# Half-block products of a two-FFN kernel: another form of the seven products, and their x operands made on VectorE

## The chip, the cores and the metric

The kernel runs on one core of a Trainium2 chip (trn2). The metric is the device time of one execution in microseconds (us), the median of several runs. The kernel before the change took 1739.53 us (three runs, 1736.28 to 1740.06).

## The reference, cut to what matters

```python
x = attention(q, k, v)               # chunks of 64 tokens, brought to 4608 tokens x 512
h = x @ w_in                         # first FFN: 512 -> 2048
r = maximum(h, 0); x = (s * r * r + b) @ w_out
h = x @ w2_in                        # second FFN: 512 -> 2048
g = h * (1 / (1 + exp(-1.702 * h)))
return g @ w2_out                    # 2048 -> 512, fp32
```

All is fp32. The kernel gets fp32 accuracy from TensorE by splitting each operand into a high part (rounded to TensorE's fp32r format) and a low part (the rest). A product of two split operands then takes three matmuls: low by high, high by high, high by low.

## The kernel before, in words

**Stages.** The 4608 tokens are nine blocks of 512. Attention and the first FFN run first; the first FFN's results go to DRAM (`y_dram`). Of the second FFN, block 0 is done in the plain way, and blocks 1 to 8 are done as four pairs by the class `Halves`. The four pairs are the program's last part, and the change touches only them.

**One pair.** A pair of token blocks and the weights are cut into halves, so that a matrix product becomes a 2 by 2 by 2 product of halves. Instead of eight half products it is made of seven, M1 to M7, of sums of halves (a form of Strassen's method). The sums of weights are made beforehand and lie in DRAM (`wi_sums`, `wo_sums`). The pair has two such products: the *first product* (x by w2_in, then the gate) and the *second product* (g by w2_out). In each, every one of the seven products M is 8 slices (`i`) by 2 times 3 matmuls of 128x512, so a pair has 2 x 336 matmuls of that size, and the four pairs 2688.

**First product** (`first`, `keep`, `quarter`, `gate`). Per slice `i` the seven products are accumulated in PSUM banks. M6 and M7 go on in the bank in which M1 was, and M3 in M5's. Between two products of one bank, ScalarE copies the bank's interim sum to SBUF (`keep`, L549) so that VectorE can add it later. The four quarters of g, "11", "12", "22" and "21", are each made of an addition from a bank (L562, L564, L568, L566), a sigmoid on ScalarE (L553) and a multiplication on VectorE (L554).

**Second product** (`operand`, `second`, `keep_out`, `result`). For each M and each `i`, an operand is split: the high part on ScalarE (L616), the low part on VectorE (L617), the sum of g halves that a later M needs on VectorE (L621, L623, L625, L627). Then six matmuls follow (L647), three for each output half `z`. Results are added on VectorE (L662, L664, L668, L670), transposed (L673) and written by SyncE (L677).

**x operands** (`load_x`, `x_split`, `operands_x`). For each half `k`, four tiles `xr` of 256 KB are loaded (L477). ScalarE makes the high parts (L492), GpSimd the low parts (L493) and the sums of halves (L502, L505, L508, L511). This work for the next pair lies in the second product of this pair, 24 and 15 plan units ahead.

**What sets the order.** Every step is entered with `at(time, step)`, a planned time in units of one product of a slice, and the steps are emitted in the order of these times. Every engine then works through its own instructions in their order, and a tile scheduler places waits on semaphores between engines. SyncE (SP) issues all DMAs in one queue: weights for the first product (`load_wi`, L520), for the second (`load_wo`, L600), and x (L477). A load into a buffer waits in that queue until the buffer is free. Buffers are few: 12 weight buffers `wi`, 7 operand buffers (3 `gh`/`gl`, 4 `op`), 10 `tmp`, and 8 PSUM banks (two "h", two "at", four "acc").

Of the kernel before, what the change touches and what calls it, by code (L numbers as in the profile page):

```python
# [16 lines left out]
P = 128  # L17
# [41 lines left out]
def chunk_attention_two_ffn(ctx, tc, q, k, v, w1_in, w1_out, s, b, w2_in, w2_out, out):  # L59
# [404 lines left out]

    class Halves:
# [24 lines left out]
        def x_split(self, m, k, src):  # L490
            self.x[m, k] = hi, lo = self.x_place(len(self.x))
            nc.scalar.activation(out=hi, in_=src, func=AF.Copy)  # L492
            nc.gpsimd.tensor_tensor(out=lo, in0=src, in1=hi.bitcast(F32), op=ALU.subtract)  # L493

        def operands_x(self, k):

            b11, b12, b22, b21 = (self.raw[k, a, c] for (a, c) in ((0, 0), (0, 1), (1, 1), (1, 0)))
            self.x_split("M1", k, b11)
            self.x_split("M2", k, b21)
            self.x_split("M3", k, b22)  # L500
            yield
            nc.gpsimd.tensor_tensor(out=b11, in0=b12, in1=b11, op=ALU.subtract)  # L502
            self.x_split("M5", k, b11)
            yield
            nc.gpsimd.tensor_tensor(out=b12, in0=b22, in1=b12, op=ALU.subtract)  # L505
            self.x_split("M7", k, b12)
            yield
            nc.gpsimd.tensor_tensor(out=b22, in0=b22, in1=b11, op=ALU.subtract)  # L508
            self.x_split("M6", k, b22)
            yield  # L510
            nc.gpsimd.tensor_tensor(out=b21, in0=b22, in1=b21, op=ALU.subtract)  # L511
            self.x_split("M4", k, b21)
# [10 lines left out]

        def first(self, i, m):

            key = {"M6": "M1", "M7": "M1", "M3": "M5"}.get(m, m)
            start = key == m
            if start:
                u = 2 * (i % 2)
                self.ps[i, key] = {  # L530
                    "M1": lambda: h_ps.tile([P, NB_MAX], F32, tag="h", name="m1"),
                    "M5": lambda: at_ps.tile([P, NB_MAX], F32, tag="at", name="m5"),
                    "M2": lambda: acc_ps.tile([P, NB_MAX], F32, tag=f"acc{u}", name="m2"),
                    "M4": lambda: acc_ps.tile([P, NB_MAX], F32, tag=f"acc{u + 1}", name="m4"),
                }[key]()
            w = self.wi[i][PLACE[m]]
            for k in range(HK):
                xh, xl = self.x[m, k]
                hi, lo = w[:, k, 0, :], w[:, k, 1, :]
                for a, (l_, r_) in enumerate(((lo, xh), (hi, xh), (hi, xl))):  # L540
                    nc.tensor.matmul(  # L541
                        out=self.ps[i, key], lhsT=l_, rhs=r_,
                        start=start and k == 0 and a == 0, stop=k == HK - 1 and a == 2,
                        skip_group_check=not start,
                    )

        def keep(self, i, m, name):
            self.kept[i, name] = t = tmp("kept")
            nc.scalar.copy(out=t, in_=self.ps[i, m])  # L549

        def gate(self, h):
            r = tmp("r")
            nc.scalar.activation(out=r, in_=h, func=AF.Sigmoid, scale=1.702)  # L553
            nc.vector.tensor_tensor(out=h, in0=h, in1=r, op=ALU.mult)  # L554

        def quarter(self, i, name):
            one, two = self.g[i]
            g = {"11": one[:, 0, :], "12": one[:, 1, :], "22": two[:, 0, :], "21": two[:, 1, :]}[name]
            ps = {m: self.ps[i, m] for m in ("M1", "M2", "M4", "M5") if (i, m) in self.ps}
            kept = {n: self.kept[i, n] for n in ("M1", "M5", "M16", "M167") if (i, n) in self.kept}  # L560
            if name == "11":
                nc.vector.tensor_tensor(out=g, in0=ps["M2"], in1=kept["M1"], op=ALU.add)  # L562
            elif name == "12":
                nc.vector.tensor_tensor(out=g, in0=ps["M5"], in1=kept["M16"], op=ALU.add)  # L564
            elif name == "21":
                nc.vector.tensor_tensor(out=g, in0=kept["M167"], in1=ps["M4"], op=ALU.subtract)  # L566
            else:
                nc.vector.tensor_tensor(out=g, in0=ps["M1"], in1=kept["M5"], op=ALU.add)  # L568
            self.gate(g)
# [4 lines left out]
        def plan_first(self):  # L574
            self.wi = {}

            def load(i):
                self.w = {}
                self.load_wi(i)
                self.wi[i] = self.w  # L580
            for i in range(HF):
                t = self.base + 3.5 * i
                at(t - 9, load, i)
                at(t, self.rooms_g, i)
                for n, m in enumerate(IN_ORDER):
                    at(t + 0.5 * n, self.first, i, m)
                at(t + 0.6, self.keep, i, "M1", "M1")
                at(t + 1.1, self.keep, i, "M5", "M5")
                at(t + 1.6, self.quarter, i, "11")
                at(t + 2.1, self.keep, i, "M1", "M16")  # L590
                at(t + 2.6, self.quarter, i, "12")
                at(t + 3.6, self.quarter, i, "22")
                at(t + 3.55, self.keep, i, "M1", "M167")
                at(t + 3.65, self.quarter, i, "21")
# [10 lines left out]
        def operand(self, n, i):  # L605
            m = OUT_ORDER[n]
            one, two = self.g[i]
            b11, b12, b22, b21 = one[:, 0, :], one[:, 1, :], two[:, 0, :], two[:, 1, :]
            src = {"M1": b11, "M2": b21, "M3": b22, "M5": b11, "M6": b22, "M7": b12, "M4": b21}[m]
# [9 lines left out]

            if m == "M1":  # L620
                nc.vector.tensor_tensor(out=b11, in0=b12, in1=b11, op=ALU.subtract)  # L621
            elif m == "M2":
                nc.vector.tensor_tensor(out=b12, in0=b22, in1=b12, op=ALU.subtract)  # L623
            elif m == "M3":
                nc.vector.tensor_tensor(out=b22, in0=b22, in1=b11, op=ALU.subtract)  # L625
            elif m == "M6":
                nc.vector.tensor_tensor(out=b21, in0=b22, in1=b21, op=ALU.subtract)  # L627
# [3 lines left out]
        def second(self, n, i):  # L631
            m = OUT_ORDER[n]
            key = {"M6": "M1", "M7": "M1", "M3": "M5"}.get(m, m)
            start = key == m
            hi, lo = self.op.pop((n, i))
            w = self.wo[n, i // 2]
            for z in range(2):
                if start and i == 0:
                    self.ps[key, z] = {
                        "M1": lambda: acc_ps.tile([P, NB_MAX], F32, tag=f"acc{z}", name="m1"),  # L640
                        "M5": lambda: at_ps.tile([P, NB_MAX], F32, tag="at", name="m5"),
                        "M2": lambda: h_ps.tile([P, NB_MAX], F32, tag="h", name="m2"),
                        "M4": lambda: acc_ps.tile([P, NB_MAX], F32, tag=f"acc{2 + z}", name="m4"),
                    }[key]()
                wh, wl = (w[:, i % 2, z, part, :] for part in range(2))
                for a, (l_, r_) in enumerate(((wl, hi), (wh, hi), (wh, lo))):
                    nc.tensor.matmul(  # L647
                        out=self.ps[key, z], lhsT=l_, rhs=r_,
# [4 lines left out]
        def keep_out(self, z):  # L653
            self.kept[z] = t = tmp("kept")
            nc.scalar.copy(out=t, in_=self.ps["M5", z])

        def result(self, name, z):
            ps = self.ps
            c = tmp("c")
            if name == "11":  # L660
                nc.vector.tensor_copy(out=c, in_=ps["M1", z])
                nc.vector.tensor_tensor(out=c, in0=ps["M2", z], in1=c, op=ALU.add)  # L662
            elif name == "12":
                nc.scalar.copy(out=c, in_=ps["M1", z])  # L664
                nc.vector.tensor_tensor(out=c, in0=ps["M5", z], in1=c, op=ALU.add)
            elif name == "21":
                nc.scalar.copy(out=c, in_=ps["M1", z])
                nc.vector.tensor_tensor(out=c, in0=c, in1=ps["M4", z], op=ALU.subtract)  # L668
            else:
                nc.vector.tensor_tensor(out=c, in0=ps["M1", z], in1=self.kept[z], op=ALU.add)  # L670
# [11 lines left out]
        def plan_second(self):  # L682
            self.wo = {}
            base = self.base + 3.5 * HF
            for n, m in enumerate(OUT_ORDER):
                for r in range(HF // 2):
                    at(base + 4 * n + r - 9, self.load_wo, n, r)
                for i in range(HF):
                    t = base + 4 * n + 0.5 * i
                    at(t - 1.8, self.operand, n, i)  # L690
                    at(t, self.second, n, i)
                done = base + 4 * n + 4
                for z in range(2):
                    if m == "M5":
                        at(done + 0.1, self.keep_out, z)
                    if m == "M2":
                        at(done + 0.1, self.result, "11", z)
                    if m == "M6":
                        at(done + 0.1, self.result, "12", z)
                    if m == "M7":  # L700
                        at(done + 0.1, self.result, "21", z)
                        at(done + 0.2, self.result, "22", z)
# [81 lines left out]
```

## Time and profile before

| | |
|---|---|
| median of three runs | 1739.53 us |
| the profiled execution's own time | 1740.82 us |
| its span (first to last instruction) | 1739.0 us |
| mean granted TensorE clock | 0.967 of full speed |
| busy: TensorE matmuls (PE) | 1623.5 us, 93%, 8864 matmuls |
| busy: VectorE (DVE) | 1236.7 us, 71% |
| busy: ScalarE (ACT) | 738.5 us, 42% |
| busy: GpSimd (POOL) | 485.0 us, 28% |

The shares are means over all stages. The pairs take the stretch from 1051.7 us to the end of the span. In that stretch the busy shares differ between the first products and the second ones, so it is read piece by piece. Matmuls overlap in TensorE's pipeline, so their listed durations (0.39 us) are longer than the step from one to the next; the step is what counts. In the trace a start time is in us from the span's start.

### The profile page before, as it was taken

The numbers are of one execution on the slowest core, as the hardware profiler recorded it, in microseconds if no ns is written. First come the engines' busy times: TensorE is split into PE (matmuls) and PEld (weight loads), VectorE is DVE, ScalarE is ACT, GpSimd is POOL, SyncE is SP. The second block draws the span as 40 slices with busy tenths as digits, with TensorE's granted clock in tenths as the row PEclk, the third lists the DMA queues.
The fourth block names the chain that finished last, engine by engine and source line by source line (L and its number), as shares of the span: only waits on it lengthen the run. The fifth ranks groups of instructions, "written<-read, shape, count | busy, mean of one in ns | idle before, by whom it ended". The sixth has DMA issues, their size and how long they took to land.

```text
span 1739.0 us, 24721 instructions
## 1 busy us (share of the span) xinstructions
PE 1623.5 (93%) x8864; PEld 1317.1 (76%) x8864; DVE 1236.7 (71%) x1804; ACT 738.5 (42%) x1226; POOL 485.0 (28%) x398
## 2 busy tenths in 40 slices
PE   4767999999999999999999999988999899889997
PEld 3555788888878888888888888776877687768785
DVE  6999876868787776868633324779568956885684
ACT  3545533334333433333344424554346334633552
POOL 3677422223222223222234313034004400430000
PEclk7888999999999999999999999998999899999998
DMA  8723454655555556644243424674767576757662
GB/s 188 200 79 87 104 129 122 152 134 148 128 155 130 137 137 162 168 122 128 79 128 97 130 77 146 198 243 117 224 193 242 144 202 188 240 151 204 191 214 53
DMA packets 407130, 263.81 MB, mean 152 GB/s; under 512 B 264160, under 2 KB 354272, under 8 KB 407008
## 3 DMA queue, kind: packets, MB, share of 16 engines
q1 hardware_dynamic: 407008, 262.23, 54.4%
q8 instruction: 70, 1.15, 0.3%
q14 instruction: 52, 0.43, 0.1%
HBM read 205.52 MB, written 56.62 MB: 151 GB/s over the span
## 4 chain that ended last, share of the span: by engine, by line
PE 71%; DVE 18%; DMA 4%; ACT 2%; issue 2%; SPq 2%; POOL 1%; DVEq 0%; ACTq 0%; POOLq 0%
PE acc L445 19%; PE h L402 19%; PE m L541 16%; PE m L647 13%; DVE pt L299 2%; DVE wo L625 1%; DVE op L617 1%; PE xT L307 1%; PE sc L273 1%; DVE r L411 1%; DVE gl L617 1%; DVE wo L568 1%; DVE wo L627 1%; DMA xr<-y 1%; ACT kept L549 1%
## 5 line engine op out<-in xcount | busy, mean ns | idle before, releaser
L402 PE MATMUL h<-xh,wi 128*128 128x512 f32 x1280 | 401.8, 396 | 8.8 <-ACT r L410 6.1
L445 PE MATMUL acc<-gh,wo 128*128 128x512 f32 x1152 | 361.0, 397 | 21.4 <-ACT gh L415 13.0
L402 PEld LDWEIGHTS h<-xh,wi 128*128 128x128 f32 x1280 | 242.4, 191 | 61.2 <-issue 9.4
L445 PEld LDWEIGHTS acc<-gh,wo 128*128 128x128 f32 x1152 | 218.0, 191 | 68.3 <-issue 9.5
L402 PE MATMUL h<-xl,wi 128*128 128x512 f32 x640 | 251.5, 394 | 0.0
L445 PE MATMUL acc<-gl,wo 128*128 128x512 f32 x576 | 224.8, 393 | 2.4 <-POOL gl L416 2.4
L411 DVE SCALAR_TENSOR_TENSOR r<-r,sb 128x512 f32<-128x512 f32 x144 | 135.8, 943 | 106.0 <-ACT r L410 105.5
L647 PE MATMUL m<-op,wi 128*128 128x512 f32 x768 | 194.7, 403 | 14.6 <-DVE op L617 12.2
L647 PEld LDWEIGHTS m<-op,wi 128*128 128x128 f32 x768 | 147.1, 194 | 53.2 <-DVE op L617 19.8
L419 DVE SCALAR_TENSOR_TENSOR gl<-r,sb,gh 128x512 fp32r<-128x512 f32 x128 | 127.3, 995 | 69.7 <-ACT gh L418 69.5
L541 PE MATMUL m<-xh,wi 128*128 128x512 f32 x512 | 160.8, 395 | 2.6 <-DVE wo L568 0.8
L418 ACT ACTIVATE gh<-r,sb 128x512 fp32r<-128x512 f32 x128 | 92.6, 724 | 165.8 <-DVE r L411 165.2
L493 POOL TENSOR_TENSOR xl<-xr,xh 128x512 fp32r<-128x512 f32 x32 | 49.3, 1557 | 399.1 <-PE m L647 259.1
L410 ACT ACTIVATE r<-h 128x512 f32<-128x512 f32 x144 | 85.1, 591 | 153.3 <-PE h L402 147.1
L402 PEld LDWEIGHTS h<-xl,wi 128*128 128x128 f32 x640 | 122.1, 191 | 25.9
L140 POOL TENSOR_TENSOR wm<-wm,wc 128x512 int32<-128x512 int32 x42 | 61.8, 1470 | 264.4 <-DVE wm L136 103.6
L299 DVE STREAM_TRANSPOSE pt<-p 32x256 f32<-32x256 f32 x288 | 125.6, 436 | 4.8
L553 ACT ACTIVATE r<-wo 128x512 f32<-128x512 f32 x128 | 80.7, 631 | 112.6 <-DVE wo L562 51.0
L445 PEld LDWEIGHTS acc<-gl,wo 128*128 128x128 f32 x576 | 108.5, 189 | 26.2 <-POOL gl L416 3.2
L647 PE MATMUL m<-gh,wi 128*128 128x512 f32 x384 | 119.7, 404 | 3.7 <-DVE wo L566 3.7
L554 DVE TENSOR_TENSOR wo<-wo,r 128x512 f32<-128x512 f32 x128 | 87.3, 691 | 46.4 <-ACT r L553 43.5
L617 DVE TENSOR_TENSOR op<-wo,op 128x512 fp32r<-128x512 f32 x128 | 99.7, 793 | 28.1 <-ACT op L616 28.0
(113 smaller groups left out, 2597.9 us busy)
## 6 DMA issues: line engine op xcount, KB each, us to landing
wi<-wo_sums SPq DMA_DIRECT2D x112, 512.0 KB, 4.1
wi<-wi_sums SPq DMA_DIRECT2D x96, 512.0 KB, 3.7
wi_sums<-wst SPq DMA_DIRECT2D x32, 448.0 KB, 3.6
wo_sums<-wst SPq DMA_DIRECT2D x32, 448.0 KB, 3.5
wst<-in_moe_w_in SPq DMA_DIRECT2D x21, 512.0 KB, 4.6
wst<-in_moe_w_out SPq DMA_DIRECT2D x21, 512.0 KB, 4.1
y<-ost SPq DMA_DIRECT2D x36, 256.0 KB, 3.1
wi<-wi_sums SPq DMA_DIRECT2D x32, 256.0 KB, 3.6
```

The costliest lines, as they stand in the source:

```text
L299: nc.vector.transpose(out=pt[r.start + ek * BK:r.start + (ek + 1) * BK, :, eq * BK:(eq + 1) * BK], in_=p[r.start + eq * BK:r.start + (eq + ...
L402: nc.tensor.matmul(out=ps, lhsT=w_[:, kk, :], rhs=x_, start=kk == 0 and a == 0, stop=kk == KD - 1 and a == 2,)
L410: nc.scalar.activation(out=r, in_=ps, func=AF.Relu)
L411: nc.vector.scalar_tensor_tensor(out=r, in0=r, scalar=s_ap, in1=r, op0=ALU.mult, op1=ALU.mult)
L418: nc.scalar.activation(out=gh, in_=r, func=AF.Identity, bias=b_ap)
L419: nc.vector.scalar_tensor_tensor(out=gl, in0=r, scalar=b_ap, in1=gh.bitcast(F32), op0=ALU.add, op1=ALU.subtract)
L445: nc.tensor.matmul(out=acc[m], lhsT=l_, rhs=r_, start=i == 0 and a == 0, stop=i == KF - 1 and a == 2)
L541: nc.tensor.matmul(out=self.ps[i, key], lhsT=l_, rhs=r_, start=start and k == 0 and a == 0, stop=k == HK - 1 and a == 2, skip_group_check= ...
L553: nc.scalar.activation(out=r, in_=h, func=AF.Sigmoid, scale=1.702)
L554: nc.vector.tensor_tensor(out=h, in0=h, in1=r, op=ALU.mult)
L617: nc.vector.tensor_tensor(out=lo, in0=src, in1=hi.bitcast(F32), op=ALU.subtract)
L647: nc.tensor.matmul(out=self.ps[key, z], lhsT=l_, rhs=r_, start=start and i == 0 and a == 0, stop=i == HF - 1 and a == 2, skip_group_check= ...
```

## The change

It has three parts, all in the class `Halves`.

1. The 22 subtractions per pair that make x operands (14 low parts, 8 sums of halves) run on VectorE instead of GpSimd.
2. Another form of the seven products: M1, M6, M7 and M4 all accumulate in one bank ("x", one of the four "acc" banks, number `i % 4`), M5 and M3 in a bank "d", M2 in a bank "b". Per slice ScalarE keeps three interim sums instead of four. The quarter "21" is now the bank "x" itself: its sigmoid and its multiplication read PSUM, and no addition is needed. The quarter "12" gets a subtraction of "11" behind it, which takes the place of the eight subtractions that followed M1's operands; M7's operand is M1's quarter after M6's subtraction.
3. The order and the times: the second product runs M1, M5, M6, M2, M7, M3, M4, the first product by a table of times (M4 of a slice comes behind two products of the next); operands are planned 3 units ahead instead of 1.8; of the results, "11" comes after M2, "22" after M7, "12" after M3, and "21" after M4, transposed straight from PSUM. Six copies of interim sums go to ScalarE, and there are no copies on VectorE.

The core of the diff:

```diff
-IN_ORDER = ("M1", "M5", "M2", "M6", "M3", "M4", "M7")
-OUT_ORDER = ("M1", "M5", "M2", "M3", "M6", "M4", "M7")
+BANK = {"M1": "x", "M6": "x", "M7": "x", "M4": "x", "M5": "d", "M3": "d", "M2": "b"}
+OUT_ORDER = ("M1", "M5", "M6", "M2", "M7", "M3", "M4")
...
+    def minus(to, one, two):
+        nc.vector.tensor_tensor(out=to, in0=one, in1=two, op=ALU.subtract)
...
-            nc.gpsimd.tensor_tensor(out=lo, in0=src, in1=hi.bitcast(F32), op=ALU.subtract)
+            nc.vector.tensor_tensor(out=lo, in0=src, in1=hi.bitcast(F32), op=ALU.subtract)
...
             self.x_split("M1", k, b11)
+            minus(b12, b12, b11)
+            yield
+            self.x_split("M5", k, b12)
+            minus(b12, b22, b12)
...
+        def bank(self, key, bank, *tags):
+            pool, tag = {"x": (acc_ps, tags[0]), "d": (at_ps, "at"), "b": (h_ps, "h")}[bank]
+            self.ps[key] = pool.tile([P, NB_MAX], F32, tag=tag, name=bank)
...
         def first(self, i, m):
+            key = i, BANK[m]
+            start = key not in self.ps
             if start:
+                self.bank(key, BANK[m], f"acc{i % KD}")
...
+        def quarter(self, i, name):
+            if name == "21":
+                h = self.ps[i, "x"]
+            else:
+                ps, kept = {"11": ("b", "M1"), "12": ("d", "M16"), "22": ("x", "M5")}[name]
+                h = g
+                nc.vector.tensor_tensor(out=h, in0=self.ps[i, ps], in1=self.kept[i, kept], op=ALU.add)
             r = tmp("r")
             nc.scalar.activation(out=r, in_=h, func=AF.Sigmoid, scale=1.702)
-            nc.vector.tensor_tensor(out=h, in0=h, in1=r, op=ALU.mult)
+            nc.vector.tensor_tensor(out=g, in0=h, in1=r, op=ALU.mult)
+            if name == "12":
+                minus(g, g, one[:, 0, :])
...
+                for n, m in ((0, "M1"), (0.5, "M5"), (1.5, "M6"), (2, "M2"), (2.5, "M3"), (3, "M7"), (4.5, "M4")):
+                    at(t + n, self.first, i, m)
...
         def second(self, n, i):
+                start = m in ("M1", "M5", "M2")
                 if start and i == 0:
+                    self.bank(key, BANK[m], f"acc{HK + z}")
...
+            if name == "21":
+                c = self.ps["out", z, "x"]
...
-                    at(t - 1.8, self.operand, n, i)
+                    at(t - 3, self.operand, n, i)
                     at(t, self.second, n, i)
-                done = base + 4 * n + 4
+                done = base + 4 * n + 4.1
                 for z in range(2):
+                    if m in ("M1", "M5", "M6"):
+                        at(done, self.keep_out, z, BANK[m], {"M6": "M16"}.get(m, m))
+                    else:
+                        at(done, self.result, {"M2": "11", "M7": "22", "M3": "12", "M4": "21"}[m], z)
```

How the change moves instructions is seen in the order of an engine's instructions: line, operation, out<-in, shape, xcount for repeated ones, and the engines or DMA queues on whose semaphores it waits.

TensorE where the second product of the first pair starts, before. `m1_10530` is M1's bank for z = 0 and `m1_10534` that for z = 1; `m1_10355` is a bank of the first product.

```order
L647 MATMUL m1_10530<-gh_10484,wi_10320 128x512 [waits DMAHW6_49,DVE_49]
L647 MATMUL m1_10530<-op_10550,wi_10362 128x512 [waits DMAHW0_49]
L541 MATMUL m1_10355<-xh_9508,wi_10164 128x512 [waits Activation_49]
L647 MATMUL m1_10530<-op_10580,wi_10390 128x512 [waits DMAHW1_49,Activation_49]
L647 MATMUL m1_10530<-op_10580,wi_10390 128x512 [waits DVE_49]
L647 MATMUL m1_10534<-gh_10484,wi_10320 128x512 [waits DVE_49]
```

The same place after the change. `x_10411` is the bank of the last slice (i = 7), `x_10505` M1's bank for z = 0 and `x_10509` that for z = 1.

```order
L542 MATMUL x_10411<-xh_9554,wi_10222 128x512 [waits Activation_49]
L637 MATMUL x_10505<-gh_10429,wi_10295 128x512 [waits DMAHW6_49,DVE_49]
L637 MATMUL x_10505<-gh_10455,wi_10315 128x512 [waits DMAHW7_49]
L637 MATMUL x_10505<-op_10471,wi_10315 128x512 x3
L637 MATMUL x_10505<-op_10482,wi_10341 128x512 [waits DMAHW0_49]
L637 MATMUL x_10505<-op_10513,wi_10362 128x512 [waits DMAHW1_49]
L542 MATMUL x_10411<-xh_9562,wi_10220 128x512 [waits DVE_49]
L637 MATMUL x_10509<-gh_10429,wi_10295 128x512 [waits DVE_49]
```

After the change, M1 for z = 0 (21 matmuls there) is followed by the first product's last M4 and then by M1 for z = 1. The latter's bank is acc3, which is also the bank of slice 7 (7 % 4 = 3), so its first matmul waits for VectorE's last reading of `x_10411`.

VectorE at that place before: quarters of the last slice (`wo_10433`, `wo_10434`) and low parts of second-product operands.

```order
L568 TENSOR_TENSOR wo_10434<-m1_10435,kept_10470 128x512 [waits Activation_49]
L566 TENSOR_TENSOR wo_10434<-kept_10540,m4_10502 128x512
L617 TENSOR_TENSOR gl_10695<-wo_10433,gh_10694 128x512 [waits PE_49,Activation_49]
L617 TENSOR_TENSOR gl_10707<-wo_9888,gh_10706 128x512 [waits PE_49,Activation_49]
L554 TENSOR_TENSOR wo_10434<-wo_10434,r_10543 128x512 [waits Activation_49]
```

VectorE there after the change. `wo_10410<-x_10411,r_10570` is the multiplication of quarter "21" of slice 7, the last reading of that bank; the rows L497 and L467 with `xl` and `xr` are x operands of the next pair.

```order
L561 TENSOR_TENSOR wo_10410<-x_10411,kept_10447 128x512 [waits PE_49]
L564 TENSOR_TENSOR wo_10409<-wo_10409,r_10501 128x512 [waits Activation_49]
L467 TENSOR_TENSOR wo_10409<-wo_10409 128x512 [waits DVE_49]
L564 TENSOR_TENSOR wo_10410<-wo_10410,r_10519 128x512 [waits Activation_49]
L497 TENSOR_TENSOR xl_10633<-xr_10551,xh_10632 128x512 [waits DMAHW1_49,Activation_49]
L467 TENSOR_TENSOR xr_10553<-xr_10553,xr_10551 128x512 [waits DMAHW2_49]
L497 TENSOR_TENSOR xl_10676<-xr_10553,xh_10675 128x512 [waits Activation_49]
L564 TENSOR_TENSOR wo_10410<-x_10411,r_10570 128x512 [waits Activation_49]
L467 TENSOR_TENSOR xr_10553<-xr_10555,xr_10553 128x512 [waits DMAHW3_49,DVE_49]
```

After the change, three x instructions stand on VectorE ahead of that multiplication, the first of which waits for a load of x. These x instructions were GpSimd's before.

SyncE's queue around the loads of x for the second pair, before and then after.

```order
L600 DMA wi_10727<-wo_sums_138 128x1024 [waits DMAHW6_49,PE_49]
L477 DMA xr_10572<-y3_142 128x512 [waits DMAHW7_49,DVE_49,Pool_49]
L477 DMA xr_10574<-y4_143 128x512 [waits DMAHW0_49,DVE_49]
L477 DMA xr_10576<-y4_143 128x512 [waits DMAHW1_49,DVE_49]
L477 DMA xr_10578<-y3_142 128x512 [waits DMAHW2_49,DVE_49]
L600 DMA wi_10756<-wo_sums_138 128x1024 [waits DMAHW3_49,PE_49]
```

```order
L597 DMA wi_10549<-wo_sums_138 128x1024 [waits DMAHW0_49,PE_49]
L481 DMA xr_10551<-y3_142 128x512 [waits DMAHW1_49,DVE_49,Activation_49]
L481 DMA xr_10553<-y4_143 128x512 [waits DMAHW2_49,DVE_49]
L481 DMA xr_10555<-y4_143 128x512 [waits DMAHW3_49,DVE_49]
L481 DMA xr_10557<-y3_142 128x512 [waits DMAHW4_49,DVE_49]
L597 DMA wi_10583<-wo_sums_138 128x1024 [waits DMAHW5_49,PE_49]
```

The loads of x stand six weight loads earlier in the queue than before, right behind the load of `wi_10549`, which waits on TensorE for a buffer that the first product's last M7 reads.

## Rows read from the trace of the kernel before

**Rows 1.** The page's part 4: the chain that ended last, by line.

```profile
PE acc L445 19%; PE h L402 19%; PE m L541 16%; PE m L647 13%; DVE pt L299 2%; DVE wo L625 1%; DVE op L617 1%; PE xT L307 1%; PE sc L273 1%; DVE r L411 1%; DVE gl L617 1%; DVE wo L568 1%; DVE wo L627 1%; DMA xr<-y 1%; ACT kept L549 1%
```

**Rows 2.** Instructions of two matmul lines: duration ns, then first and last start.

```profile
L541 PE MATMUL m<-xh,wi x512: 386/390/505, 1051.7 to 1663.1; 128*128 128x512 f32 x171
...
L647 PE MATMUL m<-op,wi x768: 387/390/797, 1129.5 to 1726.1; 128*128 128x512 f32 x192
```

**Rows 3.** The chain of waits: start us, us, what; three runs of matmuls.

```profile
1056.85 23.59 PE m L541 x104
...
1081.88 8.48 PE m L541 x36
...
1091.80 8.51 PE m L541 x36
```

**Rows 4.** Windows: stretch, length, busy us (x instructions) by engine, PEclk, DMA share, GB/s.

```profile
1160.00:1193.00 33.00, 24.31 (x82) 17.27 (x81) 31.45 (x25) 15.18 (x28) 29.72 (x18) 0.84 0.45 146
...
1226.00:1300.00 74.00, 73.47 (x318) 58.90 (x317) 50.69 (x78) 34.79 (x61) 0.00 (x0) 1.00 0.69 201
...
1335.00:1365.00 30.00, 22.42 (x69) 15.67 (x67) 29.96 (x24) 11.27 (x20) 27.24 (x17) 0.77 0.39 121
...
1508.00:1538.00 30.00, 20.14 (x68) 13.57 (x67) 29.96 (x25) 11.29 (x20) 26.43 (x16) 0.89 0.38 116
```

**Rows 5.** Timeline of DVE, then of POOL, in the first of these stretches.

```profile
1167.23 1.77 DVE L617 TENSOR_TENSOR op<-wo,op 128x512 fp32r<-128x512 f32 x1
1168.93 1.77 DVE L627 TENSOR_TENSOR wo<-wo 128x512 f32<-128x512 f32 x1
...
1168.41 1.74 POOL L493 TENSOR_TENSOR xl<-xr,xh 128x512 fp32r<-128x512 f32 x1
```

**Rows 6.** Timeline of DVE in the second pair's first product, where POOL rests.

```profile
1265.63 0.68 DVE L623 TENSOR_TENSOR wo<-wo 128x512 f32<-128x512 f32 x1
1266.23 0.68 DVE L562 TENSOR_TENSOR wo<-m,kept 128x512 f32<-128x512 f32 x1
```

**Rows 7.** Instructions of two DVE lines: duration ns min/median/max, first and last start.

```profile
L625 DVE TENSOR_TENSOR wo<-wo x32: 676/1168/1775, 1165.6 to 1691.3; 128x512 f32<-128x512 f32 x32
...
L662 DVE TENSOR_TENSOR c<-m,c x8: 677/678/683, 1182.4 to 1692.5; 128x512 f32<-128x512 f32 x8
```

**Rows 8.** The chain of waits at the start of the first pair's second product.

```profile
1132.72 0.60 ACT kept L549
...
1133.34 0.69 DVE wo L568
1134.03 0.60 DVE wo L566
```

**Rows 9.** Loads of x: landing of all; of two bursts, with the median.

```profile
DMA to landing us min/median/max: 4.6/6.7/8.1
...
xr<-y SPq DMA_DIRECT2D x4, 256.0 KB, 7.2
...
xr<-y SPq DMA_DIRECT2D x4, 256.0 KB, 5.0
```

**Rows 10.** Instructions of two ACT lines, the high part of x and the sigmoid.

```profile
L492 ACT ACTIVATE xh<-xr x32: 613/631/636, 991.7 to 1516.8; 128x512 fp32r<-128x512 f32 x32
...
L553 ACT ACTIVATE r<-wo x128: 615/632/637, 1062.0 to 1667.2; 128x512 f32<-128x512 f32 x128
```

**Rows 11.** Windows inside the first stretch of rows 4.

```profile
1170.50:1174.10 3.60, 0.22 (x1) 0.00 (x0) 3.60 (x4) 2.24 (x5) 3.60 (x3) 0.87 0.47 148
1174.10:1180.00 5.90, 5.46 (x12) 3.68 (x12) 5.90 (x5) 1.46 (x3) 5.90 (x4) 0.50 0.00 1
...
1183.40:1186.80 3.40, 3.40 (x10) 2.59 (x9) 3.40 (x4) 1.16 (x2) 2.26 (x3) 0.50 0.00 0
```

**Rows 12.** Timeline of the end of the program.

```profile
1727.93 8.67 SPq L677 DMA_DIRECT2D out<-ost  x16
...
1731.15 0.71 DVE L673 STREAM_TRANSPOSE ost<-c 128x512 f32<-128x512 f32 x1
```

More of the change, by code (lines that the diff above doesn't have):

```diff
@@ L498, in operands_x @@
             self.x_split("M1", k, b11)
+            minus(b12, b12, b11)
+            yield
+            self.x_split("M5", k, b12)
+            minus(b12, b22, b12)
+            yield
+            self.x_split("M6", k, b12)
+            minus(b11, b12, b11)
+            yield
             self.x_split("M2", k, b21)
+            minus(b21, b21, b12)
+            yield
+            self.x_split("M7", k, b11)
             self.x_split("M3", k, b22)
[L501 to L511, printed above, removed]
             self.x_split("M4", k, b21)
@@ L545, in first, with keep @@
                     )
[L547 to L553, printed above, removed]
-            nc.vector.tensor_tensor(out=h, in0=h, in1=r, op=ALU.mult)
+        def keep(self, key, name):
+            self.kept[key[0], name] = t = tmp("kept")
+            nc.scalar.copy(out=t, in_=self.ps[key])
         def quarter(self, i, name):
@@ L584, in plan_first @@
                 at(t, self.rooms_g, i)
[L585 to L591, printed above, removed]
+                for n, m in ((0, "M1"), (0.5, "M5"), (1.5, "M6"), (2, "M2"), (2.5, "M3"), (3, "M7"), (4.5, "M4")):
+                    at(t + n, self.first, i, m)
+                at(t + 0.6, self.keep, (i, "x"), "M1")
+                at(t + 1.1, self.keep, (i, "d"), "M5")
+                at(t + 2.1, self.keep, (i, "x"), "M16")
+                at(t + 2.6, self.quarter, i, "11")
+                at(t + 3.1, self.quarter, i, "12")
                 at(t + 3.6, self.quarter, i, "22")
-                at(t + 3.55, self.keep, i, "M1", "M167")
-                at(t + 3.65, self.quarter, i, "21")
+                at(t + 5.1, self.quarter, i, "21")
         def load_wo(self, n, r):
@@ L607, in operand @@
             one, two = self.g[i]
-            b11, b12, b22, b21 = one[:, 0, :], one[:, 1, :], two[:, 0, :], two[:, 1, :]
-            src = {"M1": b11, "M2": b21, "M3": b22, "M5": b11, "M6": b22, "M7": b12, "M4": b21}[m]
+            b11, t1, b22, b21 = one[:, 0, :], one[:, 1, :], two[:, 0, :], two[:, 1, :]
+            src = {"M1": b11, "M2": b21, "M3": b22, "M5": t1, "M6": t1, "M7": b11, "M4": b21}[m]
             if self.n_ops % 7 < 3:
@@ L618, in operand @@
             self.op[n, i] = hi, lo
[L620 to L621 removed]
+            if m == "M5":
+                minus(t1, b22, t1)
+            elif m == "M6":
+                minus(b11, t1, b11)
             elif m == "M2":
[L623 to L627, printed above, removed]
+                minus(b21, b21, t1)
         n_ops = 0
@@ L651, in second, with keep_out @@
                     )
-        def keep_out(self, z):
-            self.kept[z] = t = tmp("kept")
-            nc.scalar.copy(out=t, in_=self.ps["M5", z])
+        def keep_out(self, z, bank, name):
+            self.kept[z, name] = t = tmp("kept")
+            nc.scalar.copy(out=t, in_=self.ps["out", z, bank])
         def result(self, name, z):
[L658 to L668, printed above, removed]
-            else:
-                nc.vector.tensor_tensor(out=c, in0=ps["M1", z], in1=self.kept[z], op=ALU.add)
+            if name == "21":
+                c = self.ps["out", z, "x"]
+            else:
+                ps, kept = {"11": ("b", "M1"), "12": ("d", "M16"), "22": ("x", "M5")}[name]
+                c = self.kept[z, kept]
+                nc.vector.tensor_tensor(out=c, in0=self.ps["out", z, ps], in1=c, op=ALU.add)
             o = tmp("ost").rearrange("p (u l) -> p u l", l=BK)
```

43 lines of the change are left out of this document (5 added, 38 removed).

## The prediction

> **What bounds the kernel now.** I read the chain that ended last first, by line [rows 1]. The reader is to see that the pairs' part of it is TensorE's (L541 16%, L647 13%) with pieces of VectorE (L625, L617, L627) in between. Next I asked how long the pairs' matmuls must take. They run from 1051.7 to 1726.1 [rows 2], 674.4 us. In an unbroken run 104 of them take 23.59 us, 0.2268 each [rows 3]. There are 2688, and 12 of an earlier stage lie among them: 2700 x 0.2268 = 612.3 us. So **62.1 us of that stretch are lost**, and 12.9 more lie between the last matmul and the end of the span (1739.0).
>
> Where they go is read from the windows by stage [rows 4]. In three stretches, one in the second product of each of the first three pairs, TensorE does 82, 69 and 68 matmuls in 33, 30 and 30 us: 14.4 + 14.3 + 14.6 = 43.3 us lost. VectorE is busy there for 31.4, 30.0 and 30.0 us, thus nearly always, and GpSimd for about 27 to 30. In a stretch without GpSimd (1226 to 1300) VectorE is busy for 50.69 of 74 us and TensorE for 73.47.
>
> The timeline shows why [rows 5]: while GpSimd makes x operands, each subtraction of two SBUF tiles takes 1.77 us on VectorE and 1.74 on GpSimd, and VectorE starts one each 1.70 us (1167.23 to 1168.93). Without GpSimd it takes 0.68, and the next starts 0.60 later [rows 6]. L625 shows both ends, 0.68 to 1.78 us [rows 7], while L662, one of whose inputs is in PSUM, stays at 0.68 throughout. So in these stretches VectorE is the bound, and what slows it is GpSimd beside it.
>
> **The change part by part.**
>
> *x operands to VectorE.* Removed: 22 GpSimd subtractions per pair, 66 in the three pairs that have this work in a second product (the first pair's lie earlier, in a stretch where I cost the move at nothing, since TensorE has other blocks' matmuls ready). A VectorE and a GpSimd operation together took 1.70 us; two on VectorE take 2 x 0.60 = 1.20. A second product then has on VectorE 56 low parts, 24 sums of g, 22 x operations, 6 additions and 8 transposes: 116 x 0.60 = 69.6 us, against 336 x 0.2268 = 76.2 us on TensorE. TensorE is the longer one, so the three stretches' 43.3 us go. At 0.69 an operation, the longest that rows show for one without GpSimd, VectorE would need 80 us and lose 3.8 per pair. No row shows an x operation on VectorE; nearest are the equal SBUF subtractions at 0.60, so I take that, with 0.69 as the other end.
>
> *Four products in one bank.* Before, TensorE loses at slice hand-overs: from 1081.88 to 1091.80 it has 42 matmuls, 9.53 us, and needs 9.92, so 0.39 a slice [rows 3], about 2.4 in a first product. After, by the order, three products of other banks lie between M1 and M6 and between M6 and M7 (4.1 us), and one between M7 and M4 (6 x 0.2268 = 1.36 us). The addition that must read the bank in between takes 0.69 [rows 8], with the matmul's tail (0.39 less 0.23) and two issues about 0.95: covered. At one place per pair (slice 6) M7 and M4 stand back to back: 0.95 lost. I leave in one of the old hand-overs, 0.4. The two steps give 1.35 per pair. An edit with one answer goes with it: a copy fewer on ScalarE per slice and an addition exchanged for a subtraction on VectorE, off the path, since neither engine fills the first product.
>
> Here a rule speaks against the change. The trace shows a price of a hand-over only where ScalarE's copy (0.60) and VectorE's addition (0.69) follow each other [rows 8]. The Trainium skill, PSUM — Partial Sum Buffer, "PSUM bank collisions raise a hardware error", says that two engines on one bank must be held apart by semaphores since the hardware doesn't arbitrate; so each product in the shared bank waits for its reader. By that rule the fourth product adds eight waits per pair; were none covered, 32 x 0.95 = 30 us would be lost. By the order it is covered, and the sum goes by that.
>
> *The start of the second product.* This is a **new wait**. Let P be the end of the last M7. By the order, TensorE then has 21 matmuls of M1 (z = 0) and 6 of M4: 27 x 0.2268 = 6.1 us. M1 for z = 1 waits for VectorE's multiplication of quarter 21, slice 7, because both use acc3. That multiplication stands on VectorE behind three x operations, and these wait for a load of x. That load stands in SP's queue behind a weight load that waits for P, so it is issued at about P + 0.6. Loads of x land 4.6 to 8.1 us after issue, median 6.7, bursts 5.0 and 7.2 [rows 9]; I take 6.2, nearer the quieter burst, as fewer weight loads are in flight there. Then come: high part 0.63, low part and sum 2 x 0.60, second high part 0.63, sigmoid 0.63 [rows 10], multiplication 0.69, with hand-overs 4.1. TensorE goes on at P + 0.6 + 6.2 + 4.1 = P + 10.9, thus **4.8 us late** (3.2 with a landing of 4.6, 6.7 with 8.1). Queued behind the waiting low part are the next low parts of g, but those have M1 z = 1's matmuls ahead of them.
>
> After a hold the clock may fall: behind 3.6 us in which one matmul ran, the granted clock was 0.50, the lower of the two levels (1.2 of 2.4 GHz); 12 matmuls took 5.9 us, 3.2 too long; another such piece did 10 in 3.4, 1.1 too long [rows 11]. I take 2.0 per hold. So 6.8 per pair in the first three pairs. The fourth has no next pair: its multiplication needs only sigmoid, multiplication and issues behind M4, 1.6.
>
> *The end.* Four results become two, and these are transposed straight from PSUM. Now 16 DMA issues take 8.67 us, 0.54 each, and the span ends 2.4 after them [rows 12]. After, the last matmul starts at E; z = 0's transposes start before it, so the 8 issues start at about E + 0.5, end at E + 4.8, and the span at E + 7.2 instead of E + 12.9: **5.7 less**. A transpose from PSUM is not in the trace; I take the 0.71 of one from SBUF [rows 12]. An addition that reads PSUM costs 0.68 like one that doesn't [rows 6, 7], so I see no end that moves the sum by more than 0.1.
>
> **Sum.** Loss in the pairs after: 3 x (1.35 + 6.8) + 1.35 + 1.6 = 27.4 instead of 62.1, thus 34.7 less; with the end 40.4 less. The profiled execution took 1740.8 (span 1739.0 and 1.8 around it): 1700.4. It lies 1.3 above the median of the runs, so I predict **1699 us**. The forecast's own range, from a landing of 8.1 (+5.7) and some operations at 0.65 to short holds, is 1692 to 1709.
>
> **Rivals.**
>
> *A. The new wait is short and the clock stays up.* With the landing of 4.6 the hold is 3.2, and without the clock's 2.0 each pair saves 3.6 more: 1699 - 3 x 3.6 = **1688**. For it: one load burst landed in 5.0. Against: the loads run beside 512 KB weight loads, and the hold is then hardly shorter than the one behind which the clock fell [rows 11]. The Trainium skill, DMA: Bandwidth & Descriptors, "Anatomy of one DMA — SWDGE (gpsimd) path", gives a fixed part of about 2.0 us plus the bytes at 436 GB/s, which for 256 KB is an estimate of 2.6 us; no load of x here landed so early. Were the hold only the fourth pair's 1.6 with no clock lost: 1699 - 3 x 5.2 = 1683.
>
> *B. VectorE becomes the bound of the second product.* The x work is a chain in turn on ScalarE and VectorE. If VectorE stands for each of 8 high parts and their hand-overs (0.7 each, 5.6 us per pair) and an operation costs 0.65: 116 x 0.65 + 5.6 = 81.0 against 76.2, 4.8 lost per pair, 1699 + 14.4 = **1713**; at 0.69 even 1727. For it: VectorE has only 9% to spare over the whole product and the x work lies in one half of it. Against: the operands are planned earlier (3 units), and in a stretch without GpSimd it kept TensorE at 99% [rows 4].
>
> *C. The shared bank decides: slower.* If at each M7 to M4 the reader is late (behind other VectorE work in its queue), TensorE stands there 28 times. The place is the addition of quarter 22. It decides from 1.45 us per hand-over on, where 28 x 1.45 = 40.6 eats all of the gain; at 1.8 it gives 28 x 1.8 = 50, **1749**. It needs the addition to end 3.2 us after M7. For it: every x bank waits twice for VectorE. Against: VectorE was busy for only 69% of a first product [rows 4].
>
> *D. The change doesn't do what it says*: VectorE's slow subtractions had another cause than GpSimd, for instance DMA traffic, so 1.70 stays, and now 22 more come. It would come out near **1740**. Against: L625's shortest and longest differ by exactly GpSimd's presence [rows 6, 7].
>
> **How the numbers follow.** Forecast 0.62, A 0.14, B 0.18, C 0.04, D 0.02. The range of 8 in 10 takes in the forecast, most of A and the nearer half of B: 1683 to 1717. Two runs of this kernel can be told apart from about 0.2% on, 3.5 us. Faster by more than that: forecast, A and B, 0.94; within: D, 0.02; slower: C, 0.04.
>
> **What would show it.** In the profile after: no GpSimd work beyond about 1050 us; VectorE's subtractions at 0.68 throughout; windows in the middle of a second product with TensorE at 99%; a hold of 3 to 7 us about 6 us into each of the first three second products, released by the multiplication of L564, with a granted clock of 0.5 behind it; the first products within 1.5 us of 76.2; and 7 us between last matmul and end. The forecast is wrong if VectorE is busy through a second product with TensorE waiting for low parts of g (L615 in the changed kernel, B), or if TensorE's holds in first products are released again and again by the additions of quarters (L561 there, C).

## The result, and the profile after

The changed kernel took **1697.38 us** (median of four runs, 1696.16 to 1698.30) against 1739.41 before: a ratio of 0.9761, 95% interval 0.9745 to 0.9778. The forecast was 1699, its own range 1692 to 1709.

The profiled execution (1696.5 us of span, 1739.0 before) is best read in three pieces, by the start times of matmuls:

| piece | before | after | difference | forecast |
|---|---|---|---|---|
| up to the pairs' first matmul | 1051.7 | 1049.9 | -1.8 | 0 |
| first to last matmul of the pairs | 674.4 | 639.5 | -34.9 | -34.7 |
| last matmul's start to the end | 12.9 | 7.1 | -5.8 | -5.7 |

The first line is no effect of the change that I can name: in eight more kernels, alike up to the pairs but for the first pair's x work, the pairs began between 1048.4 and 1051.9. The other two are 40.7 us against a forecast of 40.4.

The page of the changed kernel, engines and chain by line. GpSimd is 139 us lighter (485.0 before), and the VectorE lines L617, L625 and L627 of [rows 1] have no successors among the lines of the chain that the page lists:

```profile
PE 1603.6 (95%) x8864; PEld 1317.1 (78%) x8864; DVE 1198.1 (71%) x1844; ACT 722.8 (43%) x1194; POOL 345.6 (20%) x310
...
PE acc L446 21%; PE h L403 21%; PE x L637 10%; PE x L542 10%; PE d L637 5%; PE d L542 5%; PE b L637 3%; PE b L542 2%; DVE pt L300 2%; PE xT L308 2%; PE sc L274 1%; DVE r L412 1%; DMA xr<-y 1%; DMA wst<-in_moe_w_in 1%; SPq L246 1%
```

Windows of the changed kernel (columns as in [rows 4]): the middle of the first and the second pair's second product, and between them a first product. These answer to [rows 4]:

```profile
1145.00:1191.00 46.00, 46.00 (x205) 38.06 (x204) 44.78 (x75) 28.08 (x49) 0.00 (x0) 1.00 0.72 221
1211.00:1289.00 78.00, 77.22 (x341) 63.61 (x340) 44.88 (x68) 33.70 (x59) 0.00 (x0) 1.00 0.73 218
1304.00:1351.00 47.00, 47.00 (x208) 38.86 (x207) 45.88 (x77) 29.48 (x52) 0.00 (x0) 1.00 0.73 224
```

In the middle pieces TensorE now never rests, where before it did 82 matmuls in 33 us. VectorE is just as full as before (44.78 of 46, 45.88 of 47), but it does 75 instructions there where it did 25 in 33 us. The sums of halves in the changed kernel, by instruction, answer to L625 in [rows 7]:

```profile
L467 DVE TENSOR_TENSOR wo<-wo x128: 676/682/693, 1067.6 to 1650.3; 128x512 f32<-128x512 f32 x128
```

None of 128 takes over 0.69 us. Next, the new wait: the chain of waits of the changed kernel at the start of the first pair's second product (start us, us, what):

```profile
1129.13 6.32 DMA xr<-y
...
1135.48 0.64 ACT xh L496
...
1136.14 0.69 DVE xl L497
1136.83 0.61 DVE xr L467
...
1137.47 0.64 ACT xh L496
...
1138.13 0.52 DVE xl L497
...
1138.74 0.69 DVE wo L564
...
1139.47 8.11 PE x L637 x25
```

The load lands 6.32 us after its issue (6.2 was taken), then come high part (L496), low part (L497), sum (L467), high part, low part and the multiplication of L564, 4.0 us where the forecast had 4.1. The forecast counted the sigmoid where the chain names the second low part; it ran beside that on ScalarE:

```profile
1138.00 0.58 ACT L563 ACTIVATE r<-x 128x512 f32<-128x512 f32 x1
```

Then TensorE goes on with M1 for z = 1. From the start times of the matmuls, this hold is 4.83 us, in the second and third pair 5.15 and 5.04, in the fourth 1.57 (forecast 4.8 and 1.6). Windows around it, the same columns:

```profile
1134.40:1139.40 5.00, 0.40 (x2) 0.00 (x0) 2.56 (x5) 1.75 (x3) 0.00 (x0) 0.78 0.56 188
1139.40:1144.04 4.64, 4.57 (x11) 3.60 (x12) 4.61 (x9) 3.70 (x7) 0.00 (x0) 0.50 0.13 24
```

Behind the hold the granted clock is 0.50, that is 1.2 of 2.4 GHz, and 11 matmuls take 4.64 us where 20 fit.

The end of the program after the change, DVE and SP (answering to [rows 12]):

```profile
1689.13 1.40 DVE L656 STREAM_TRANSPOSE ost<-x 128x512 f32<-128x512 f32 x2 [6.60 <-PE x L637]
1689.88 4.14 SPq L660 DMA_DIRECT2D out<-ost  x8
```

Two transposes straight from the bank and 8 DMA issues, 7.1 us from the last matmul's start (1689.4) to the end (1696.5).

### The profile page after: what moved, and what is told of

The parts are those of the page before. It is cut to its first block, busy times and chain, and to the rows that moved or that the text cites. A ratio compares the mean times of both kernels' runs of the same rounds, so it can differ in the third digit from the quotient of the medians.

```text
span 1696.5 us, 24510 instructions
## 1 busy us (share of the span) xinstructions
PE 1603.6 (95%) x8864; PEld 1317.1 (78%) x8864; DVE 1198.1 (71%) x1844; ACT 722.8 (43%) x1194; POOL 345.6 (20%) x310
## 4 chain that ended last, share of the span: by engine, by line
PE 79%; DVE 12%; DMA 3%; SPq 2%; ACT 1%; issue 1%; POOL 0%; DVEq 0%; ACTq 0%; POOLq 0%
PE acc L446 21%; PE h L403 21%; PE x L637 10%; PE x L542 10%; PE d L637 5%; PE d L542 5%; PE b L637 3%; PE b L542 2%; DVE pt L300 2%; PE xT L308 2%; PE sc L274 1%; DVE r L412 1%; DMA xr<-y 1%; DMA wst<-in_moe_w_in 1%; SPq L246 1%
## 5 line engine op out<-in xcount | busy, mean ns | idle before, releaser
L614 ACT ACTIVATE op<-wo 128x512 fp32r<-128x512 f32 x128 | 79.9, 631 | 80.9 <-PE x L637 27.8
L564 DVE TENSOR_TENSOR wo<-wo,r 128x512 f32<-128x512 f32 x96 | 66.0, 691 | 63.4 <-ACT r L563 62.9
L637 PE MATMUL x<-op,wi 128*128 128x512 f32 x432 | 104.9, 390 | 0.0
L542 PE MATMUL x<-xh,wi 128*128 128x512 f32 x320 | 99.6, 391 | 3.3 <-DVE wo L561 3.1
L637 PEld LDWEIGHTS x<-op,wi 128*128 128x128 f32 x432 | 81.7, 189 | 17.3
L563 ACT ACTIVATE r<-wo 128x512 f32<-128x512 f32 x96 | 60.7, 633 | 76.5 <-DVE wo L561 75.8
L615 DVE TENSOR_TENSOR op<-wo,op 128x512 fp32r<-128x512 f32 x128 | 85.3, 680 | 7.4 <-ACT op L614 6.0
L467 DVE TENSOR_TENSOR wo<-wo 128x512 f32<-128x512 f32 x128 | 85.7, 684 | 0.8
```

The lines of the kernel that those rows point to most:

```text
L467: nc.vector.tensor_tensor(out=to, in0=one, in1=two, op=ALU.subtract)
L542: nc.tensor.matmul(out=self.ps[key], lhsT=l_, rhs=r_, start=start and k == 0 and a == 0, stop=k == HK - 1 and a == 2, skip_group_check=not ...
L615: nc.vector.tensor_tensor(out=lo, in0=src, in1=hi.bitcast(F32), op=ALU.subtract)
L637: nc.tensor.matmul(out=self.ps[key], lhsT=l_, rhs=r_, start=start and i == 0 and a == 0, stop=i == HF - 1 and a == 2, skip_group_check=not ...
```

## The experiments

Eight kernels were run. "Loss" below is the time of a stretch less 0.2268 us per matmul in it, from start times.

| kernel | median us | ratio to before, 95% interval |
|---|---|---|
| x subtractions on VectorE, else as before | 1704.04 | 0.9805 (0.9788 to 0.9822) |
| changed kernel, x subtractions on GpSimd | 1736.08 | 0.9988 (0.9978 to 0.9997) |
| changed kernel, other bank for M1 | 1679.79 | 0.9669 (0.9651 to 0.9687) |
| changed kernel, x loaded earlier | 1689.53 | 0.9718 (0.9699 to 0.9736) |
| changed kernel, lead 1.8 | 1697.81 | 0.9773 (0.9758 to 0.9787) |
| changed kernel, low parts of x twice | 1705.69 | 0.9808 (0.9793 to 0.9822) |
| other bank, x 2 units earlier | 1677.70 | 0.9648 (0.9632 to 0.9664) |
| other bank, x 4 units earlier | 1680.36 | 0.9665 (0.9650 to 0.9679) |

**One: only the engine of the x work.** The kernel before, with

```diff
-            nc.gpsimd.tensor_tensor(out=lo, in0=src, in1=hi.bitcast(F32), op=ALU.subtract)
+            nc.vector.tensor_tensor(out=lo, in0=src, in1=hi.bitcast(F32), op=ALU.subtract)
```

and the same in the four sums of `operands_x`.

> The kernel before with one thing changed: the 22 x subtractions per pair run on VectorE instead of GpSimd; form, banks and order stay. Theory (GpSimd's operations beside VectorE's are what stretched these to 1.70 us): no VectorE subtraction of the pairs over 0.75 us, and most of the 43 us of the three middle stretches go. This form needs 128 VectorE operations in a second product, 128 x 0.60 = 76.8 us against TensorE's 76.2, so some 10 to 15 us stay: 1705 to 1716. Rival (the new form and order freed the stretches, or the stretch has another cause than GpSimd): 1730 or more, with L617 and L625 still at 1.7 us.

Measured: 1704.04, a little under the range given. Windows of this kernel in the first pair's second product, and L625 there:

```profile
1150.00:1172.00 22.00, 22.00 (x99) 18.13 (x98) 19.53 (x34) 14.65 (x27) 0.00 (x0) 1.00 0.92 315
1172.00:1186.00 14.00, 10.82 (x43) 7.38 (x42) 14.00 (x24) 5.73 (x10) 0.00 (x0) 1.00 0.61 155
```

```profile
L625 DVE TENSOR_TENSOR wo<-wo x32: 674/682/692, 1163.4 to 1652.2; 128x512 f32<-128x512 f32 x32
```

L625, 1.78 us at its longest before, is 0.69 at its longest, with the line, its operands and the form of the seven products untouched: GpSimd beside it was the cause. The DMA share beside it is even higher (0.92) than in the slow stretches of [rows 4]. What stays is a piece of 14 us in which VectorE is busy throughout and TensorE does 43 matmuls: 128 operations are one more than TensorE's 76.2 us hold at 0.60 (127). The Trainium skill, SBUF — State Buffer, "Who interferes with whom", states that a VectorE instruction with two SBUF inputs contends with a GpSimd one that reads SBUF, and one with at most one SBUF input, outside the 2-port modes, does not. The trace agrees: 1.70 against 0.60 a step, while L662, with one input in PSUM, stayed at 0.68 [rows 5 to 7], also where a GpSimd subtraction ran beside it (kernel before):

```profile
1182.37 0.68 DVE L662 TENSOR_TENSOR c<-m,c 128x512 f32<-128x512 f32 x1
...
1181.98 1.62 POOL L505 TENSOR_TENSOR xr<-xr 128x512 f32<-128x512 f32 x1
```

**Two: only the form.** The changed kernel with the 22 subtractions back on GpSimd (`nc.gpsimd` in `x_split` and for the four sums in `operands_x`).

> The changed kernel with the x subtractions back on GpSimd; form, banks, order and lead stay. Theory: the 1.70 us operations come back in the second products of the first three pairs, some 11 to 14 us lost in each, less 2 to 4 for the wait at the start of the second product, since VectorE no longer stands behind a load of x there: 1715 to 1730. Rival (the form and the longer lead carry the gain): within 5 us of 1697.

Measured: 1736.08, outside the range: the theory's direction, but more came back than expected. The loss in the second products is 20.6, 20.4 and 18.6 us, the wait at their start included. Timeline of this kernel, DVE then POOL, and its chain of waits:

```profile
1150.12 1.75 DVE L618 TENSOR_TENSOR op<-wo,op 128x512 fp32r<-128x512 f32 x1
...
1149.62 1.71 POOL L470 TENSOR_TENSOR xr<-xr 128x512 f32<-128x512 f32 x1
```

```profile
1141.63 3.48 DVE gl L618 x2
...
1145.11 5.09 DVE wo L467 x3
1150.20 1.67 DVE op L618
...
1155.30 2.85 PE d L640 x8
...
1183.73 1.55 issue
1185.29 1.74 DVE wo L467
1187.03 1.68 DVE gl L618
```

VectorE steps at 1.70 us again, and this time in two bursts per pair, as the loads of the two halves come apart; in the first two pairs the granted clock fell to 0.50 once in each burst. The range took 11 to 14 us per pair for this, but these rows show VectorE on the path from 1141.6 on, with nothing to cover it. The wait at the start shrank to 3.3, 3.0 and 2.5 us only, since the sigmoid on ScalarE still stood behind a high part of x that waits for the load.

The first two kernels and the two given ones make a square: with x on GpSimd the new form brings 2.6 us (1738.69 to 1736.08), with x on VectorE 6.7 (1704.04 to 1697.38); the move to VectorE brings 34.7 with the old form and 38.7 with the new. (1738.69 is the kernel before in these experiments' session; it was 1739.41 in the changed kernel's, and by the intervals each of these differences is known to some 3 to 4 us.) The end of the program alone gives 5.9 of the form's share (12.97 us in experiment one, 7.09 after the change). So **in the pairs themselves the new form gained nothing**: the loss there is 26.2 us in experiment one's profiled execution and 27.1 after the change. It saved 1.3 us in each first product (losses 2.3 to 2.6 against 1.1 to 1.5) and what VectorE lacked in the second, and gave it back in the wait for the bank. Without that wait the same form does bring something: experiment three, below, is 24.3 us faster than experiment one.

**Three: another bank.** The changed kernel with M1 for z = 0, 1 in the second product in acc1 and acc2:

```diff
-                    self.bank(key, BANK[m], f"acc{HK + z}")
+                    self.bank(key, BANK[m], f"acc{1 + z}")
```

> The changed kernel with M1's banks in the second product moved from acc2 and acc3 to acc1 and acc2, so that M1 for z = 1 no longer shares a bank with slice 7 of the first product. The planner then also orders the instructions there anew (x operands later on VectorE). Theory (the 5 us wait of each second product is one for that bank): the waits and the half clock behind them go, some 7 us in each of three pairs and 1.6 in the fourth: 1672 to 1680. Rival (TensorE needs VectorE's work there in any case, and the wait comes back at the next low part): 1688 to 1700.

Measured: 1679.79, at the upper end of the theory's range. Neither hold nor half clock is left at the starts of the second products, and the 0.95 of the back-to-back M7 and M4 is gone too: the planner now puts M1 of the second product between them, and a first product loses nothing that the start times show. The planner's new order is not what frees TensorE: the multiplication of quarter 21, slice 7, comes later than before, 1151.44 where it was 1138.74, and no matmul waits for it:

```profile
1151.44 0.67 DVE L564 TENSOR_TENSOR wo<-x,r 128x512 f32<-128x512 f32 x1
```

Windows of the first pair's second product:

```profile
1120.00:1135.00 15.00, 15.00 (x68) 12.41 (x67) 9.54 (x15) 8.26 (x16) 0.00 (x0) 1.00 0.62 180
1135.00:1174.00 39.00, 37.63 (x167) 30.82 (x165) 39.00 (x66) 24.23 (x43) 0.00 (x0) 1.00 0.84 274
1174.00:1187.00 13.00, 11.75 (x50) 9.42 (x51) 12.96 (x22) 7.80 (x15) 0.00 (x0) 1.00 0.44 134
```

Part of the rival came true: VectorE is busy without a pause from 1135 on, and late in the product TensorE waits for it, 3 us a pair, by way of copies of interim sums on ScalarE (L645) that stand behind high parts of x. With the hold gone the x work in turn on ScalarE and VectorE is the bound there, as rival B had it, at 3 us a pair instead of its 4.8.

**Four: the load earlier.** The changed kernel with

```diff
-                at(self.base + t - 3, self.load_x, k)
+                early = 8 if self.j > 1 and k == 0 else 0
+                at(self.base + t - 3 - early, self.load_x, k)
```

> The changed kernel with the four loads of x for half 0 of the next pair planned 8 units earlier (second to fourth pair); nothing else is changed, and TensorE's order there stays. Theory (the multiplication that frees the bank is late because VectorE stands at a load of x ahead of it): the wait shrinks from 5.0 to the fourth pair's 1.6 us and the clock stays up, some 5 us in each of three pairs: 1680 to 1686. Rival (VectorE then does the x work at the cost of the last quarters, and the first product's end waits instead): 1692 to 1700.

Measured: 1689.53, between the two. Its chain of waits:

```profile
1114.24 4.83 DMA xr<-y
...
1119.10 0.02 ACT xh L496
...
1119.63 0.61 ACT r L563
1120.25 0.48 ACT kept L550
...
1120.77 1.67 PE x L542 x6
...
1125.56 0.13 DVE xr L467
...
1126.07 0.69 DVE wo L561
...
1126.81 3.02 PE x L542 x12
...
1138.71 0.60 ACT r L563
...
1139.34 0.70 DVE wo L564
...
1140.08 5.05 PE x L637 x21
```

The wait at the start of the second product is now 1.57 us in all four pairs, and the clock stays at 1.00: the load ahead on VectorE made up the rest. But the first product now has two holds: 1.7 and 1.8 us in the first pair, 0.95 and 1.8 in the second, 2.1 and 1.8 in the third. The first of them is new: by the chain, a high part of x waits for the load on ScalarE, with a sigmoid and a copy of an interim sum behind it. The second is the changed kernel's own step of 0.94 us between M7 and M4, made 0.9 longer by an x operation (L467, `xr`) that stands on VectorE ahead of the addition of L561. Both theories hold, each for its part.

**Five: the lead.** `at(t - 1.8, self.operand, n, i)` in place of `at(t - 3, ...)`.

> The changed kernel with operands of the second product planned 1.8 units ahead, as before, instead of 3. Theory (TensorE bounds the second product, the lead only has to cover a stretch in which VectorE has as much work as TensorE): 1.2 units less are 1.6 us of cover less, so at most 5 us over three pairs: 1697 to 1703. Rival (the longer lead is what keeps TensorE fed in the middle): 1710 or more.

Measured: 1697.81, the changed kernel's time (1697.38), as the theory had it, but the experiment doesn't test it. From the pairs' first matmul on, all 2700 matmuls, VectorE's 704 and ScalarE's 519 instructions and SyncE's 384 DMA issues stand in both traces in the same order, by line and tile name: the planned time was changed, and what the engines do was not. So the run says how alike two executions of one order are; what a lead is worth stays open, and so does what sets how far ahead VectorE works (the seven operand buffers may).

**Six: how near VectorE is to being the bound.** `x_split` with its subtraction written twice.

> The changed kernel with each low part of x computed twice on VectorE (the same values), 14 more operations per pair. It measures how near VectorE is to being the bound. Theory (between 116 x 0.60 = 69.6 and TensorE's 76.2 us there are only 6.6 us, and the x work lies in one half of the product): 14 x 0.60 = 8.4 us more in that half, of which the lead and the slack hide some 3 to 5; 3 to 6 us per pair: 1706 to 1715. Rival (VectorE has room to spare): within 3 us of 1697.

Measured: 1705.69, 8.3 us more, 0.3 under the range, and not lost where I had put it. Window of the first pair's second product, and the chain in the next first product:

```profile
1146.00:1196.00 50.00, 50.00 (x221) 41.18 (x220) 50.00 (x84) 28.87 (x52) 0.00 (x0) 1.00 0.69 215
```

```profile
1227.24 0.50 SPq L661
...
1227.85 4.57 DMA wi<-wi_sums
...
1232.55 3.45 PE x L543 x14
```

VectorE does 84 operations in 50 us, without a pause, and TensorE is still busy for all 50. What is late are VectorE's last results: their output DMAs go out late, and a weight load behind them on SP comes 1.6 to 1.9 us too late for the next first product. So with 130 operations VectorE has nothing to spare here, and most of the price is paid through SP's queue: of the 6.4 us that the pairs of this profiled execution lose more than the changed kernel's, 5.3 are these three waits.

**Seven and eight: x earlier, with the other bank.** The other-bank kernel with `t -= 2 if self.j > 1 else 0` (and 4) ahead of the loads and steps of x.

> The other bank (acc1, acc2) with all x loads and x operations of the second to fourth pair planned 2 units earlier. Theory (in the other-bank kernel VectorE works without a pause for 53 us of a second product and falls behind by 3 us at its end; work moved ahead into its idle time at the start wins these back): 1671 to 1676. Rival (x operations ahead wait for their loads and hold up the last quarters and the first operands, as in the changed kernel): 1680 to 1690.

> The same with 4 units earlier; here the loads of x stand further ahead in the queue too. Theory: 1671 to 1676, the loads land in time. Rival (the last quarters of the first product are held up by x work): 1680 to 1690.

Measured: 1677.70 and 1680.36, both over the theory's range, and the second inside the rival's. Two units earlier leave a loss of 1.6 to 1.8 us per pair instead of 2.9 to 3.2, four units earlier leave it at 2.8 to 3.1. The rival's mechanism is not what the start times show: in both kernels the first products lose nothing, and with four units TensorE waits in the second products, for low parts of g (0.9 and 1.2 us). The gain is less than expected; VectorE is busy nearly throughout all the same, which fits but was not tested apart. Windows of the first pair, two units earlier:

```profile
1133.00:1164.00 31.00, 30.14 (x131) 24.06 (x129) 29.52 (x49) 20.48 (x38) 0.00 (x0) 1.00 0.86 295
1164.00:1184.00 20.00, 19.80 (x87) 16.40 (x88) 20.00 (x35) 12.98 (x23) 0.00 (x0) 1.00 0.63 193
```

The kernel two units earlier is the fastest that I have, 3.5% under the kernel before and 1.2% under the change; its interval overlaps with that of the other bank alone.

## Why the prediction was right, point by point

*GpSimd beside VectorE bounds the middle of the second products.* Right, and shown: experiment one removes only this and gains 34.7 us; experiment two puts it back into the changed kernel and the gain of the pairs is gone. Rival D (another cause of 1.70 us) fell with L625 in experiment one.

*116 operations x 0.60 against 76.2 us.* Right: the step stayed at 0.60, and TensorE was held nowhere in the middle. Experiment six shows how narrow this was: with 14 operations more VectorE never rests in the middle and its last results come late. Rival B was the nearest to coming true, and with the hold removed it is what remains. One of the two arguments against it carries no weight: planning the operands 3 units ahead instead of 1.8 changes nothing in the order (experiment five).

*One bank for four products.* First products lost 1.06, 1.05, 1.53 and 1.07 us against 1.35 forecast. The fourth product's hand-over is covered but for the one place that the order showed (a step of 1.17 us, 0.94 too long). Rival C, and with it the case against the change that I made of the rule on PSUM banks, has nothing in the trace; the program keeps the rule by its waits, and a product of another bank in between hides them. A late reader occurred in experiment four, where the addition came 0.9 us later and TensorE stood that much longer; hand-overs late by the 1.45 us from which C would decide were not tried, so that point stays an estimate.

*The start of the second product.* Hold and clock: losses of 7.1, 7.2 and 6.7 us against 6.8, and 1.7 in the fourth pair against 1.6. The mechanism is shown from two sides: another bank removes the hold, an earlier load shortens it to the fourth pair's 1.57. Rival A did not happen: loads of x have a median of 5.4 us in the changed kernel, and none landed under 4.0, but this one took 6.32. The estimate of 2.6 us named with rival A is for DMAs that GpSimd issues; SP issues these.

*The clock.* Behind a hold 2.0 us were taken; the losses less the holds are 2.2, 2.1 and 1.7. It is not a fixed price: in experiment two, holds of 3.3 and 3.0 us were not followed by a fall of the granted clock, and one of 2.5 us was (0.50 for 3.4 us).

*The end.* 7.1 us against 7.2.

That the sum is right to 0.3 us is in part luck: the first products lost 0.7 us less than forecast, the starts of the second products 0.7 more.

What the prediction did not see is how the gain divides between the parts. Its sum mixed the move to VectorE with the new form; only experiments one and two tell that the form by itself brings the shorter end and nothing in the pairs, as long as M1 shares acc3 with slice 7.

## What to carry to other kernels

Work on GpSimd is not free because GpSimd is idle: here a two-input subtraction on each of the two engines took 1.70 us together, and 1.20 one after the other on VectorE alone, so ask what the neighbour loses, from the durations of its instructions in the stretch where both run. When a product's accumulator moves to another bank, follow that bank to its last reader, and then ask what stands ahead of this reader in its own engine's queue; here it was a load for the next stage, and another bank number was worth 17.6 us. And when a change has parts, run them alone: the part with most lines brought the least until the bank was changed too. Before an experiment's time is read, compare the order of the engines' instructions with that of the kernel it was made from: an edit of a planned time may change nothing.

## What the runs showed that I had not expected

The edit of the lead left every engine's order as it was, so it was no experiment on the lead (1697.81 against 1697.38 us). VectorE ran for 50 us without a gap at 84 operations, 0.60 each, and TensorE did not feel it (experiment six): a fully busy engine beside the bound one need not cost anything, until its last results delay a queue.
